# A new order of steps for a fused retention and Gelu MLP kernel: 1,332 steps listed anew, casts and copies given to other engines

## Chip, cores and metric

The kernel runs on one core of one Trainium2 chip. The metric is the device time of one launch in microseconds; lower is better.

## What is computed

Eight batches of eight heads, 576 positions, head size 64. Each head's attention has no softmax: scores are multiplied by a decay that depends on the distance, and the future is cut off. The result, 4608 tokens of 512 numbers, goes through a two-layer MLP with a tanh Gelu.

```python
scores = scale * np.matmul(q, k.transpose(0, 1, 3, 2))
gamma = 1.0 - 2.0 ** (-5.0 - np.arange(H, dtype=np.float32))
Dmat = np.where(rel >= 0, gamma[:, None, None] ** rel[None, :, :], 0.0)
attn = np.matmul(scores * Dmat[None, :, :, :], v)
x = attn.transpose(0, 2, 1, 3).reshape(B * S, H * D)        # 4608 x 512
h = x @ w_in                                                # 512 x 2048
g = 0.5 * h * (1.0 + np.tanh(c * (h + 0.044715 * h * h * h)))
out = g @ w_out                                             # 2048 x 512
```

Inputs and output are f32; the matmuls run in f16.

## The kernel before

**Tiling.** A unit u is a stretch of 128 positions of one batch (the fifth of each batch has 64): 40 units, u = 5 · batch + c. The retention is computed unit by unit with a running state, so a unit needs the scores inside it and the state of those ahead. The units of two batches (0, 2, 5, 7) are loaded in pairs ("wide"). The MLP takes the tokens in nine blocks t of 512. For t = 0 it is computed plainly; the second matmul from t = 1 on and the first from t = 6 on use Strassen's scheme, with seven products of half blocks in place of eight, whose sums and assembly fall to the other engines.

**Order.** Nothing is scheduled by a program at run time. The string `ORDER` is a list of steps; a loop at the end of the kernel calls one helper for each. Every engine gets its instructions in the order in which the steps stand in the list and works them off in that order, each waiting for its own inputs. PE, DVE, ACT and POOL have a list each, and SP a list of DMA issues; weights are issued from POOL's list. A step that waits holds up all that stands behind it on its engine. The last field of a step names the engine where there is a choice: v for DVE, a for ACT, g for POOL (for `t`, o and h name the PSUM ring).

| Step | Helper | What it does |
|---|---|---|
| L,u,n | load | SP: page n (q, k, v) of unit u |
| I,g and J,g | load_w_in, load_w_out | a chunk of w_in or w_out (256 KB in f16), cast by a DMA from POOL's list. N with fc 0 to 3 needs I,0 and I,1; 4 to 7 I,2 and I,3; 8 to 11 I,4 and I,5; 12 to 15 I,6 and I,7 |
| q, k, v | cast_q, cast_k, cast_v | page to f16, q and v with their decay |
| D,u | dma_T | SP: q and k transposed by a DMA (needs both casts) |
| t, y | pe_T, copy_T | the same by PE, and the copy out of PSUM |
| X, Y, R | wide_kv, wide_scores, wide_attend | PE's work for a wide pair |
| B,u,w | attend | scores of unit u and output of unit w on PE |
| m | masked | DVE: scores times the mask |
| a, o, z | state_sum, state_decay, state_16 | running state, its decay, its f16 copy |
| x | x_out | ACT: unit's output into xT, the MLP's input |
| N, F | mm1, gelu | w_in matmul (8 of 256 columns) and its Gelu |
| O, e | mm2, result | w_out matmul for t = 0 (and the last), copy out |
| P, E, Q | mm2_cols, result_cols, store | the last 128 tokens in three parts of columns |
| T, U, s, H | sum_b, sum_w, sum_x, sum_a | Strassen's sums, on DVE |
| W, V, S | product, assemble, store | Strassen's w_out products, assembly, store |
| A, l, f | product_h, part_h, gelu_h | Strassen's w_in products, parts, Gelu |
| K,n | busy | n filler matmuls on the identity (L1003), their result is not used |
| Z, g, c, w | zero, decay_rows, constants_short, table | constants; w runs one small Gelu |

**Buffers.** PSUM gives two banks to the ring "h" (N, A, t, K), two to "o" (O, W, t), and the rest to scores and outputs. A bank comes free when its reader is done: F for N, V for W, l and f for A. The f16 sums of Strassen's second matmul lie in eight tiles `ssum`, two sets of four, which `pair` hands out to the halves pr of each block t.

Of the kernel before, what the change touches and what calls it, by code (L numbers as in the profile page):

```python
# [1075 lines left out]
```

## Time and profile before

| What | Value |
|---|---|
| Time, median of 3 runs | 297.72 us (297.13 to 298.09) |
| Span of the profiled execution, first to last instruction | 293.9 us |
| The profiled execution's own time | not listed apart; at the median, 3.8 us lie around the span |
| Granted TensorE clock | 1.000 |
| DMA, mean | 169 GB/s, 49.79 MB in 136428 packets |
| PE's work in the span, useful matmuls and 36 fillers | 280.3 us busy |
| Fillers (L1003) | 10.4 us busy |
| Gelus (L765, L975) | 56.7 + 29.5 us on ACT |
| First and last instruction of N,0,2,0 and N,0,0,0 on PE | 21.30 to 23.21 us |
| Last matmul's end | 290.85 us |

The profile's busy time of an engine says how much it worked, not what it delays. PE is busy through most stretches of ten microseconds, so what counts is where it is not: in the head, until its inputs are there, and in single holes later. A wait of another engine costs something only where PE, in turn, waits for that engine. Rows of the timeline give start, duration, engine, line, operation, and in brackets the idle time ahead and what ended it.

### The profile page before, as it was taken

To read this page: it belongs to the slowest core of one execution; us is meant where nothing else is said; L and a number is where in the kernel's file an instruction comes from. 1 tells how busy PE (TensorE), PEld (TensorE's weight loads), DVE (VectorE), ACT (ScalarE), POOL (GpSimd) and SP (SyncE) were. 2 spreads that over 40 slices of the span, in tenths; PEclk is the share of its full clock that TensorE was granted. 3 is DMA by queue.
4 is the path that set the end of the run, shared out by engine and by line. 5 is a ranking of instruction groups with operands and counts; after the bars stand their busy time and mean duration, and the time that the engine had idled before them with its cause. 6 is when DMAs were issued, how large, how long until landed. Compare 5 with 4: busy or idle time off the path is not lost.

```text
span 293.9 us, 9639 instructions
## 1 busy us (share of the span) xinstructions
PE 280.3 (95%) x4064; PEld 235.2 (80%) x4064; DVE 216.6 (74%) x447; ACT 150.1 (51%) x289; POOL 109.6 (37%) x168
## 2 busy tenths in 40 slices
PE   3797999999999999999999999999999999999995
PEld 1355886667888888888888888888888788888874
DVE  7686753696865678576678699799889988977740
ACT  2144774334634543554553646546777587665411
POOL 5931910414351084163415544783467123000000
PEclk9999999999999999999999999999999999999999
DMA  7999999997979999989099978899498370002103
GB/s 212 283 236 250 217 220 211 214 179 162 248 142 228 178 186 220 230 206 210 23 235 214 196 166 178 187 204 153 131 195 208 75 205 7 36 8 102 74 25 121
DMA packets 136428, 49.79 MB, mean 169 GB/s; under 512 B 118208, under 2 KB 130880, under 8 KB 136384
## 3 DMA queue, kind: packets, MB, share of 16 engines
q1 hardware_dynamic: 132032, 44.97, 71.3%
q0 software_dynamic: 4352, 4.20, 8.5%
q8 instruction: 32, 0.52, 0.8%
q14 instruction: 12, 0.10, 0.1%
HBM read 36.70 MB, written 9.44 MB: 157 GB/s over the span
## 4 chain that ended last, share of the span: by engine, by line
PE 86%; POOL 5%; DMA 4%; DVE 3%; issue 1%; ACT 0%; POOLq 0%; ACTq 0%
PE bank L860 30%; PE bank L757 27%; PE bank L957 12%; PE bank L783 6%; DMA w_in_sb<-in_moe_w_in_dram 4%; PE sk L553 2%; PE x L529 2%; POOL w_in_sb L238 2%; PE sk L563 1%; PE x L574 1%; PE bank L987 1%; DVE pages L817 1%; POOL wide L269 1%; PE bank L493 1%; PE x L677 1%
## 5 line engine op out<-in xcount | busy, mean ns | idle before, releaser
L757 PE MATMUL bank<-xT,w_in_sb 128*128 128x256 f16 x768 | 94.4, 273 | 2.1 <-DMA w_in_sb<-in_moe_w_in_dram 2.1
L765 ACT ACTIVATE gT<-bank 128x512 f16<-128x512 f32 x96 | 56.7, 598 | 61.5 <-PE bank L757 59.7
L757 PEld LDWEIGHTS <-w_in_sb 128*128 128x128 f16 x768 | 73.8, 98 | 13.7 <-DMA w_in_sb<-in_moe_w_in_dram 2.7
L860 PEld LDWEIGHTS <-ssum 128*128 128x128 f16 x480 | 46.3, 98 | 6.5 <-issue 0.8
L269 POOL CAST sz<-s 64x256 f16<-64x256 f32 x48 | 24.4, 509 | 66.2 <-DVE s L713 45.9
L860 PE MATMUL bank<-tsum,ssum 128*128 128x256 f16 x360 | 46.0, 273 | 0.6 <-DVE ost L817 0.6
L860 PEld LDWEIGHTS <-gT 128*128 128x128 f16 x360 | 34.8, 98 | 4.5 <-issue 0.2
L424 POOL TENSOR_TENSOR qk<-pages,dec 128x512 f16<-128x512 f32 (+1 forms) x20 | 22.2, 1122 | 32.9 <-DMA pages<-in_q_dram 17.2
L860 PE MATMUL bank<-w_out_sb,gT 128*128 128x256 f16 x240 | 31.1, 273 | 0.0
L817 DVE TENSOR_TENSOR ssum<-gT 128x1024 f16<-128x1024 f16 x30 | 23.9, 798 | 3.9 <-ACT gT L765 3.5
L424 POOL TENSOR_TENSOR v<-pages,dec 128x512 f16<-128x512 f32 (+1 forms) x20 | 20.6, 1030 | 15.3 <-DMA pages<-in_v_dram 10.4
L817 DVE TENSOR_TENSOR ost<-u,bank 128x256 f32<-128x256 f32 x45 | 18.1, 416 | 9.5 <-PE bank L860 9.4
L817 DVE TENSOR_TENSOR ssum<-gT,ssum 128x1024 f16<-128x1024 f16 x30 | 23.4, 782 | 0.2
L691 DVE TENSOR_TENSOR ret<-sk,mask 128x512 f16<-128x512 f32 (+1 forms) x32 | 19.8, 618 | 4.3 <-PE sk L563 4.0
L957 PEld LDWEIGHTS <-pages 128*128 128x128 f16 x192 | 18.4, 98 | 2.8 <-issue 0.3
L957 PE MATMUL bank<-pages 128*128 128x256 f16 x144 | 20.3, 273 | 0.3 <-ACT pages L267 0.3
L783 PE MATMUL bank<-w_out_sb,gT 128*128 128x512 f16 x80 | 19.1, 380 | 0.0
L817 DVE TENSOR_TENSOR u<-u,bank 128x256 f32<-128x256 f32 x30 | 12.4, 415 | 8.7 <-PE bank L860 5.0
L713 DVE TENSOR_TENSOR s<-s,sk 128x256 f32<-128x256 f32 x36 | 14.9, 415 | 5.0 <-PE sk L563 4.0
L593 ACT ACTIVATE xT<-x 128x512 f16<-128x512 f32 (+1 forms) x25 | 14.3, 578 | 8.0 <-PE x L574 8.0
L817 DVE TENSOR_TENSOR hc<-hc,bank 128x512 f32<-128x512 f32 x21 | 14.4, 684 | 5.0 <-PE bank L957 2.3
L267 ACT COPY hc<-bank 128x512 f32<-128x512 f32 x19 | 11.1, 585 | 12.5 <-PE bank L957 12.4
(114 smaller groups left out, 425.8 us busy)
## 6 DMA issues: line engine op xcount, KB each, us to landing
out_dram<-ost SPq DMA_DIRECT2D x35, 256.0 KB, 3.4
pages<-in_q_dram SPq DMA_DIRECT2D x32, 256.0 KB, 4.7
pages<-in_v_dram SPq DMA_DIRECT2D x24, 256.0 KB, 4.1
pages<-in_k_dram SPq DMA_DIRECT2D x24, 256.0 KB, 4.3
pages<-in_k_dram SPq DMA_DIRECT2D x4, 512.0 KB, 5.2
pages<-in_v_dram SPq DMA_DIRECT2D x4, 512.0 KB, 6.0
w_in_sb<-in_moe_w_in_dram POOLq DMA_DIRECT2D x8, 256.0 KB, 9.8
w_out_sb<-in_moe_w_out_dram POOLq DMA_DIRECT2D x8, 256.0 KB, 10.6
```

The source lines that it names most:

```text
L267: nc.scalar.copy(out=o, in_=i)
L269: (nc.vector if eng == "v" else nc.gpsimd).tensor_copy(out=o, in_=i)
L424: eng.tensor_tensor(out=out, in0=s["raw"][:, i, 0:n], in1=dec[:, i // 2, s["j"], 0:n].unsqueeze(2).to_broadcast([128, n, D]), op=ALU.mult,)
L593: nc.scalar.activation(out=xT[:, :, o : o + G * (b - a)].rearrange("c p (h s) -> c p h s", s=G), in_=x[:, a:b].rearrange("c h p s -> c p h ...
L691: nc.vector.tensor_tensor(out=ret[:, :, 0:n], in0=now["two"][:, :, 0, 0:n], in1=mask.unsqueeze(1).unsqueeze(1).to_broadcast([128, 2, n, G] ...
L713: nc.vector.tensor_tensor(out=s32, in0=state[0], in1=kv, op=ALU.add)
L757: nc.tensor.matmul(hps[:, i, :], w_in_sb[:, ct, 128 * (fc + i) : 128 * (fc + i) + 128], xT[:, ct, TB * t % XR + lo : TB * t % XR + hi], st ...
L765: nc.scalar.activation(out=gTs[t][:, fc : fc + TB // (hi - lo), lo:hi], in_=h.pop((t, fc, lo)), func=AF.Gelu_apprx_tanh, bias=0.0, scale=1.0,)
L783: nc.tensor.matmul(ops[t, tcc], gTs[t][:, ft, 128 * tcc : 128 * tcc + 128], w_out_sb[:, ft, :], start=(ft == 0), stop=(ft == NFC - 1),)
L817: (nc.vector if eng == "v" else nc.gpsimd).tensor_tensor(out=out, in0=a, in1=b, op=op)
L860: nc.tensor.matmul(p["ps", bank][:, HN * col : HN * col + HN], a[:, k], b[:, k], start=(k == 0 and i in (1, 6)), stop=(k == HK - 1), skip_ ...
L957: nc.tensor.matmul(p["ps", bank][:, n], w[:, c, 128 * n : 128 * n + 128], x[:, c], start=(n == 0 and c == 0 and i in (1, 2, 5)), stop=(c = ...
```

## The change

`ORDER` is replaced as a whole. Both lists have the same 1,332 steps in kind and number (of `K` eleven in both, with 36 fillers before and 33 after), in another order. 120 other steps that have a choice name another engine. By kind: of z thirteen go from POOL to ACT, four from DVE to ACT, four from ACT to the others, five from POOL to DVE and eight from DVE to POOL; of k nine come to ACT and four leave it; of V nine copies go from ACT to DVE; of l five go to ACT and one leaves it; of q ten go to POOL and twelve to DVE; of v nine go each way. `w`, which stood among the steps of t = 5, stands in the head. J,0 to J,7 stand farther apart. D,9 stands ahead of the loads of units 10 to 14, and L,9,1 behind L,9,0.

In `pair`, the set of `ssum` is chosen by pr, not by the number of pairs so far.

The diff, with the list cut to its head and its end:

```diff
--- before.py
+++ after.py
 ORDER = """
-L,0,1 Z,1,v L,0,0 I,2,g L,0,2 L,2,1 L,2,0 Z,2,g q,0 k,0,g I,7,g K,4 K,4 K,4 K,3 K,4 t,0,q,h L,2,2
-L,4,1 c t,0,k,h I,1,g v,0,v X,0 y,0,k,v I,0,g I,3,g a,0,1 y,0,q,v Z,3,v k,2,g K,4 K,1 Y,0,1 t,2,k,o
-m,0,1 z,0,1,a I,6,g K,4 Y,0,0 a,1,1 q,2 L,4,0 K,4 t,2,q,h m,0,0 y,2,k,a y,2,q,v I,4,g K,1 R,0 I,5,g
-x,0 Y,2,1 L,5,0 x,1 i,4,v K,3 N,0,2,0 N,0,0,0 g o,1,1 m,2,1 L,5,1 Z,4,g v,2,v F,0,2,0 N,0,12,0 Y,2,0
-F,0,0,0 z,1,1,v N,0,4,0 L,5,2 X,2 k,4,g Z,5,v q,4 F,0,12,0 F,0,4,0 t,4,k,o a,2,1 t,4,q,o a,3,1
-y,4,q,a N,0,8,0 L,4,2 z,2,1,g L,9,1 N,0,10,0 F,0,8,0 k,5,g m,2,0 L,7,1 R,2 F,0,10,0 y,4,k,v B,4,-1
-q,5 x,3 x,2 N,0,14,0 L,7,0 t,5,q,o N,0,0,1 L,7,2 J,1,g F,0,14,0 N,0,6,0 y,5,q,v J,3,g t,5,k,o
-F,0,0,1 m,4 j,1,v J,0,g L,9,0 v,5,v J,2,g L,9,2 F,0,6,0 N,0,8,1 L,10,0 N,0,12,1 k,7,v X,5 y,5,k,a
-F,0,8,1 z,3,1,g F,0,12,1 v,4,v Y,5,0 a,5,1 m,5,0 a,6,1 N,0,4,1 N,0,6,1 F,0,4,1 q,7 F,0,6,1 t,7,k,o
-y,7,k,a N,0,2,1 J,5,g J,4,g N,0,14,1 F,0,2,1 J,6,g L,10,2 B,-1,4 F,0,14,1 x,4 Y,5,1 t,7,q,h y,7,q,a
-J,7,g m,5,1 N,0,10,1 v,7,v F,0,10,1 z,5,1,g R,5 x,5 Y,7,0 o,6,1 x,6 O,0,0 O,0,4 q,10,g L,11,1
-N,1,4,0 O,0,5 N,1,14,0 F,1,4,0 m,7,0 N,1,2,0 L,12,2 O,0,1 X,7 Y,7,1 F,1,14,0 F,1,2,0 L,15,1 k,9,a
-O,0,6 O,0,2 N,1,10,0 F,1,10,0 q,9,g O,0,3 L,11,2 N,1,6,0 D,9 F,1,6,0 m,7,1 Z,0,g k,11,a a,7,1 O,0,7
-e,0,0,v a,8,1 z,6,1,v O,0,12 T,1,0,v N,1,0,0 e,0,1,a F,1,0,0 z,8,1,g z,7,1,v N,1,8,0 O,0,13 L,10,1
-N,1,12,0 R,7 B,9,-1 H,1,0,3,v v,10,v F,1,8,0 x,8 O,0,8 L,11,0 L,12,1 O,0,14 j,5,v F,1,12,0 v,11,v
-T,1,1,v q,11 k,10,g x,7 O,0,15 N,1,6,1 H,1,0,1,v L,12,0 D,10 N,1,8,1 O,0,9 F,1,6,1 T,2,0,v v,9,v
-O,0,10 e,0,3,a T,3,0,v S,0,0 N,1,14,1 F,1,8,1 H,1,0,2,v m,9 L,14,1 B,10,9 k,12,a D,11 T,2,1,v O,0,11
-a,10,0 a,10,1 e,0,2,v N,1,12,1 L,13,2 F,1,14,1 L,13,0 x,9 N,1,10,1 m,10 F,1,12,1 T,3,1,v z,10,0,g
-B,11,10 q,12,g W,1,0,1 S,0,3 v,13,v a,11,0 V,1,0,0,a a,11,1 x,10 v,12,v W,1,0,6 L,14,0 F,1,10,1
-N,1,2,1 o,11,1 q,13,g F,1,2,1 T,4,0,v D,12 W,1,0,2 L,16,1 V,1,0,1,v N,1,4,1 N,1,0,1 S,0,2 V,1,0,2,a
-z,11,0,v F,1,4,1 z,10,1,g j,2,v m,11 S,0,1 N,2,0,0 B,12,11 q,14 a,12,0 H,1,0,4,v k,15,g F,1,0,1
-F,2,0,0 W,1,0,7 L,15,0 L,14,2 N,2,8,0 T,4,1,v N,2,4,0 V,1,0,3,v H,1,1,1,v L,13,1 z,12,0,g x,11
-k,16,g H,1,1,2,v W,1,0,4 W,1,0,5 F,2,8,0 L,17,0 a,12,1 N,2,6,0 L,17,1 V,1,0,5,v L,19,0 F,2,4,0
-k,13,g D,13 V,1,0,4,v F,2,6,0 m,12 N,2,14,0 v,14,v F,2,14,0 W,1,1,1 z,11,1,g V,1,1,0,a W,1,0,3
-V,1,0,6,v L,16,0 N,2,10,0 F,2,10,0 k,14,g W,1,1,6 V,1,1,1,v N,2,12,0 z,12,1,v L,16,2 B,13,12 x,12
-L,15,2 v,15,g D,14 q,15 W,1,1,2 H,1,1,3,v m,13 N,2,2,1 V,1,1,2,a W,1,1,7 F,2,12,0 N,2,2,0 V,1,1,3,v
...
+L,0,0 Z,3,v Z,2,v Z,1,g I,7,g K,0 L,0,2 L,0,1 q,0,g I,2,g v,0,v K,5 L,2,1 K,0 k,2,g K,4 K,4 K,4 K,4
+t,0,q,h K,4 w g k,0,v I,1,g y,0,q,v X,0 a,0,1 I,0,g t,2,k,o y,2,k,v L,2,0 z,0,1,a a,1,1 L,2,2 q,2
+t,0,k,h y,0,k,a Y,0,0 m,0,0 I,3,g I,6,g L,4,1 K,2 K,5 o,1,1 Y,0,1 m,0,1 t,2,q,h y,2,q,a I,4,g R,0
+x,1 x,0 K,1 Y,2,1 N,0,2,0 F,0,2,0 m,2,1 N,0,0,0 z,1,1,g F,0,0,0 v,2,g X,2 Y,2,0 N,0,4,0 F,0,4,0
+a,2,1 z,2,1,v a,3,1 N,0,14,0 F,0,14,0 m,2,0 R,2 x,2 x,3 L,4,0 I,5,g L,5,1 c N,0,12,0 i,3,a F,0,12,0
+L,5,0 N,0,6,0 k,4,v F,0,6,0 q,4 L,5,2 Z,0,v Z,4,v z,3,1,g J,0,g k,5,g t,4,k,o y,4,k,v N,0,0,1
+F,0,0,1 Z,5,g t,4,q,o y,4,q,a L,4,2 N,0,12,1 L,7,0 F,0,12,1 N,0,2,1 N,0,6,1 F,0,2,1 B,4,-1 m,4
+F,0,6,1 t,5,k,o y,5,k,v N,0,8,1 q,5,g F,0,8,1 J,1,g L,7,1 N,0,8,0 F,0,8,0 t,5,q,o y,5,q,a N,0,10,0
+F,0,10,0 i,1,g v,5,v X,5 a,5,1 a,6,1 Y,5,0 v,4,g N,0,14,1 F,0,14,1 N,0,4,1 F,0,4,1 B,-1,4 x,4 m,5,0
+Y,5,1 k,7,v z,5,1,a J,5,g N,0,10,1 q,7,g t,7,q,h t,7,k,o j,7,g m,5,1 R,5 O,0,4 y,7,q,v y,7,k,a Y,7,0
+x,6 O,0,0 m,7,0 L,7,2 J,2,g L,9,0 J,3,g x,5 F,0,10,1 N,1,8,0 F,1,8,0 L,9,1 N,1,4,0 v,7,v Y,7,1
+F,1,4,0 L,9,2 k,9,v q,9 J,6,g D,9 o,6,1 X,7 a,7,1 N,1,2,0 F,1,2,0 N,1,0,0 J,4,g T,1,0,v O,0,1 J,7,g
+N,1,14,0 T,3,1,v F,1,0,0 O,0,5 T,2,0,v N,1,6,0 F,1,6,0 F,1,14,0 O,0,6 O,0,2 O,0,7 L,13,0 e,0,1,a
+O,0,3 a,8,1 L,10,0 N,1,10,0 z,6,1,a N,1,12,0 O,0,8 q,10 O,0,9 L,10,1 k,10,v v,9,g T,1,1,v T,2,1,v
+O,0,10 m,7,1 L,12,1 F,1,10,0 O,0,11 z,7,1,g R,7 L,10,2 e,0,0,v L,11,0 L,11,1 B,9,-1 e,0,2,v j,1,v
+F,1,12,0 H,1,0,1,v O,0,12 O,0,13 O,0,14 k,11,a O,0,15 H,1,0,2,v L,14,0 m,9 z,8,1,v x,7 x,8 N,1,6,1
+v,10,v F,1,6,1 N,1,10,1 F,1,10,1 D,10 B,10,9 x,9 H,1,0,4,v e,0,3,a L,14,1 k,14,g L,12,0 a,10,0
+N,1,4,1 q,11,g N,1,14,1 F,1,4,1 H,1,0,3,v W,1,0,1 a,10,1 L,11,2 k,12,a N,1,0,1 V,1,0,0,a F,1,14,1
+F,1,0,1 z,10,0,a W,1,0,6 m,10 L,13,1 k,13,g L,14,2 N,1,2,1 q,12 q,13 F,1,2,1 D,11 v,11,g B,11,10
+x,10 S,0,1 V,1,0,1,v W,1,0,5 L,15,0 L,16,1 a,11,0 L,12,2 N,2,14,0 v,12,g F,2,14,0 W,1,0,2 V,1,0,2,a
+z,10,1,g N,2,2,0 F,2,2,0 S,0,0 z,11,0,g L,19,1 a,11,1 N,1,8,1 F,1,8,1 T,4,1,v o,11,1 T,3,0,v W,1,0,7
+j,4,a q,14 N,1,12,1 F,1,12,1 N,2,8,0 F,2,8,0 m,11 T,4,0,v D,12 H,1,1,1,v V,1,0,3,v q,15 V,1,0,4,v
+B,12,11 m,12 D,13 N,2,4,0 a,12,0 H,1,1,2,v a,12,1 z,11,1,g j,0,v F,2,4,0 S,0,2 L,13,2 D,14 W,1,0,4
+V,1,0,5,v W,1,0,3 L,15,2 x,11 L,21,1 L,15,1 L,17,1 L,20,1 N,2,12,0 V,1,0,6,v F,2,12,0 j,3,a L,17,0
+z,12,1,a N,2,6,0 F,2,6,0 L,16,0 W,1,1,1 N,2,10,0 v,13,v z,12,0,v B,13,12 a,13,0 F,2,10,0 k,15,g
...
 """
...
         if (t, pr) not in pairs:
             if not tsum:
                 sum_tiles()
-            n = len(pairs)
-            pairs[t, pr] = dict(s=[ssum[4 * (n % 2) + i] for i in range(4)])
+            pairs[t, pr] = dict(s=[ssum[4 * pr + i] for i in range(4)])
         return pairs[t, pr]
```

## Prediction

> **What bounds the kernel now.** I read the page's busy table first, then PE's waits, PE's busy time by stretches of ten microseconds, and the timeline of the stretches that showed a hole.
>
> ```profile
> span 293.9 us, 9639 instructions
> PE 280.3 (95%) x4064; PEld 235.2 (80%) x4064; DVE 216.6 (74%) x447; ACT 150.1 (51%) x289; POOL 109.6 (37%) x168
> ```
> PE's waits (who waited for whom: us, times, longest):
>
> ```profile
> PE bank L1003 <- DVE ident L364: 4.5, 1, 4.5
> PE bank L757 <- DMA w_in_sb<-in_moe_w_in_dram: 2.1, 2, 1.6
> PE bank L1003 <- DVE qkT L269: 1.9, 1, 1.9
> ```
> PE is the bound; the first and third wait are of fillers (L1003), the second is of real work. PE's list holds the same useful matmuls in both kernels, so the time is the moment at which the first hidden block N,0,2,0 starts, plus the same PE work, plus PE's holes after it, plus the tail. The stretches (us, busy and count of PE, PEld, DVE, ACT, POOL) show where the holes are:
>
> ```profile
> 20.00:30.00 10.00, 7.61 (x118) 5.62 (x118) 7.20 (x21) 5.50 (x9) 2.01 (x4) 1.00 1.17 240
> 30.00:40.00 10.00, 10.00 (x184) 8.87 (x183) 7.89 (x10) 6.86 (x13) 8.06 (x13) 1.00 1.02 222
> ...
> 220.00:230.00 10.00, 8.95 (x126) 7.58 (x124) 9.77 (x18) 6.86 (x13) 6.62 (x8) 1.00 0.73 172
> ...
> 250.00:260.00 10.00, 9.71 (x98) 8.47 (x96) 8.13 (x18) 6.17 (x13) 0.00 (x0) 1.00 0.07 27
> ```
> From 30 us on PE misses 1.05 + 0.29, and 0.08 and 0.02 in two stretches not shown: 1.44 us. The rest is in the head; the timeline of PE (start, duration, idle before) has it:
>
> ```profile
> 20.64 0.82 PE L1003 MATMUL bank<-ident 128*128 128x512 f16 x3
> 21.30 1.91 PE L757 MATMUL bank<-xT,w_in_sb 128*128 128x256 f16 x16
> 24.85 1.05 PE L757 MATMUL bank<-xT,w_in_sb 128*128 128x256 f16 x8 [1.64 <-DMA w_in_sb<-in_moe_w_in_dram]
> ...
> 28.61 1.70 PE L757 MATMUL bank<-xT,w_in_sb 128*128 128x256 f16 x14 [0.46 <-DMA w_in_sb<-in_moe_w_in_dram]
> ```
> The first N starts at 21.30. Then PE stands for 1.64 us until weight chunk I,6 lands (for N,0,12,0) and for 0.46 until I,5 lands (for N,0,10,0): 2.10 us. The chunks go out from POOL, and the pages from SP:
>
> ```profile
> 11.14 2.15 POOL L238 DMA_DIRECT2D w_in_sb<-in_moe_w_in_dram x3
> ...
> 14.33 2.16 POOL L238 DMA_DIRECT2D w_in_sb<-in_moe_w_in_dram x3
> ...
> 40.44 1.69 SPq L215 DMA_DIRECT2D pages<-in_q_dram  x1
> ...
> 51.62 1.61 POOL L424 TENSOR_TENSOR qk<-pages,dec 128x512 f16<-128x512 f32 x2 [13.10 <-DMA pages<-in_q_dram]
> ...
> 53.69 1.68 SPq L483 DMA_TRANSPOSE qkT<-qk  x1
> ```
> The first two rows are I,1 I,0 I,3 and I,6 I,4 I,5. I,6 took 24.85 − 14.33 = 10.5 us to land, I,5 28.61 − 15.8 = 12.8. The third row is L,10,0, used 11.2 us later.
>
> The span is 293.9; the profiled execution's own time is not listed apart, so I take the median, 297.72, of which 3.8 lies around the span.
>
> **The change, part by part.** *Start of the first N.* Fillers: 36 become 33, but all stand before the first N while PE waits for others. The opening ones, 19 in 5.92 us, become 21, so t,0,q comes at 10.26 + 2 × 0.2 = 10.65 at the latest from PE's side. q,0 goes from DVE (1.23) to POOL. No row has a 1024-wide multiply on POOL; 128x256 takes 0.67 and 128x512 1.20, so 1.2 + 2 × 0.53 = 2.3; bounds 1.2 and 2 × 1.2 = 2.4. POOL: masks end 6.5, Z,1 0.52, I,7 0.74, q,0 until 10.1, I,2 until 10.8, k,2 1.04 until 11.8, then I,1 I,0 I,3 I,6 I,4 at 0.72 each: I,0 goes out at 12.55 (before: 11.86), I,6 at 14.0 (before: 14.33). Copies: y,0,q on DVE until 12.2, z,0,1 (0.83) and y,0,k (1.01) on ACT until 14.5, so Y,0,0 at 14.5; DVE does y,2,k, a,1,1 and q,2 until 15.5, m,0,0 (1.22) until 16.7, o,1,1, m,0,1 until 18.5; R,0 then runs to 19.6 (before 19.8), x,1 and x,0 (1.09) end at 20.7, and N,0,2,0 can start 0.36 later as before: 21.05. Its weights: I,0 had landed by 21.30, at most 9.4 us after its issue, so by 12.55 + 9.4 = 21.95. Between 21.05 and 21.95 I take 21.4, since in the rows x, not the weights, was last.
>
> *Holes of the head.* Before, the third block asks for I,6 and I,7, the fifth for I,4. After, the third is N,0,4,0 (I,2 and I,3, long out) behind X,2 and Y,2,0; I,6 is needed by N,0,14,0 at 21.4 + 3 × 0.87 + 0.3 + 0.33 = 24.65. By the rows it lands between 24.5 and 25.5: a hole of 0 to 0.85, I take 0.3. I,4 and I,5 are first needed by N,0,8,1, 11.8 us of PE work after the first N, at 33.5. I,5 now stands on POOL behind z,1,1 (which waits for o,1,1, 17.3) and the wide v,2 (2.3): out at 20.6, landed by 20.6 + 12.8 = 33.4. No hole; 0.9 if v,2 starts a microsecond late. Head: before 21.30 + 2.10 = 23.40; after 21.4 + 0.3 = 21.7. Gain 1.7, bounds 2.35 and −0.35.
>
> *Gelu's table.* The load moves from 20.95 to ACT's wait after the constants, where ACT stands 6.2 us until 12.41. Before, it hid: 1.28 us to 22.23, the Gelu at 22.38, its matmuls just done at 22.2, and PE's next block waited for weights anyhow. Worth 0; with the cover of those weights gone it would be 0.15. The Trainium skill ("ScalarE: Activation LUTs", What ACT_TABLE_LOAD costs) adds about 1.38 us of drain to each switch, 2.66 together, which would put up to 1.4 us on ACT. The trace disagrees: x,0 ends at 20.94, the load starts at 20.95, and 0.15 follows it.
>
> *Other engines.* Counted from the list with row durations: 13 more z on ACT (0.81), 5 more k (0.6), 4 more l (0.585), 9 fewer V (0.37): ACT +12.5 us, to 55% of the span. POOL −11, DVE −2. ACT had waits of 60 us for PE in L765 alone, so it has room; DVE, at 9.77 of 10 where the late hole is, is not loaded more (in the 50 us of PE work around that hole the list holds 50.9 us of DVE rows before, 47.2 after). I keep the 1.44 us of holes; bounds 0 (they dissolve) and 3 (twice as many).
>
> *Tail.* Before it ends O, P,0, P,1, E,1 on ACT, Q,1; after O, P,0, P,2, E,2 on ACT, Q,2: both 128 columns. P,1 (after O,8,9) needs f,8,3,3 and f,8,2,2, two Gelus of 0.63 after V,8,0,5 and l,8,3,5; they end 0.2 us ahead of it. 0; bound 0.5. The ssum line takes 4·pr instead of 4·(n%2); pairs come in turn (pr 0, then 1), so it names the same tiles: 0.
>
> Sum: 297.7 − 1.7 = 296.0.
>
> **Rivals.** *(a) DVE stuck behind a page, slower.* D,9 now stands on SP ahead of all of L,10 to L,14, where before five of these loads went out first (40.44 to 53). D,9 waits for k,9 and q,9 on DVE, behind m,7,0 and v,7: Y,7,0 at 43.4, then 1.22 + 1.27 + 0.54 + 0.42 gives 47.2; D,9 takes 1.3 to issue, L,13,0 and L,10,0 follow, out by 49.5. q,10 on DVE waits for it, and behind it queue k,10, T,1,1, T,2,1 and m,7,1 (0.69 + 0.68 + 0.84 + 0.73 + 1.22 = 4.2). R,7 needs m,7,1 and comes 39.2 us of PE work after the first N, at 60.6 (the same count puts before's R,7 at 60.9; its row says 60.65). So it costs from a landing of 56.4 on; at 58.1 the gain of 1.7 is gone, at 59.0 the kernel is slower by 0.9. With the page's median of 4.7 it lands at 54.2; with the 11.2 of the row above at 60.7: 4.3 us lost, 300.3. Against it: by then fewer weights compete. *(b) POOL's chain late, no change.* If DVE and POOL exclude each other, q,0 waits for v,0 on DVE (1.5, to 8.5) and ends at 10.8; I,0 goes out at 13.25 and lands by 22.65: the first N moves by 1.25, 297.2, with I,6 late too up to 297.9. For it: a DVE ssum of 1.42 us (mean 0.78) beside a POOL L424 at 226 us; against: the wide v on DVE (L439) took 1.50 instead of q's 1.23 beside POOL's cast at 8.66, a stretch of 0.27 only. The Trainium skill ("SBUF — State Buffer", Who interferes with whom) says an operation of DVE with two SBUF inputs and one of GpSimd that reads SBUF block each other whole; by it this case is the likely one. The two rows split on it. *(c) The late holes dissolve*, as DVE has less there: 296.0 − 1.4 = 294.6. *(d)* The new order has late holes of its own, twice the old: 297.5 and more.
>
> **How the numbers follow.** Forecast 0.50 (0.45 of it a gain over 0.9 us), (a) 0.20, (b) 0.15, (c) 0.10, (d) 0.05 counted slower. A measurement of this kernel tells about 0.3%, 0.9 us. Faster 0.45 + 0.10 = 0.55; same 0.05 + 0.15 = 0.20; slower 0.25. The range starts at 294.8, near (c), and ends at 299.3, which takes in (b), (d) and the milder half of (a).
>
> **What would show it.** Right: first N at 21.0 to 22.0, no wait of PE for w_in_sb above 0.9, R,7 about 60.6 with no hole before it, ACT near 163 us busy. Wrong: PE idle before L665 or L677 near 60 us with DVE's q,10 waiting for pages (a); first N at 22.5 or later (b); new holes of PE after 75 us (d); a tail longer than before's 3.0 us after the last matmul.

## The result, and the profile after

After takes 293.19 us in the median of four runs (292.71 to 294.13), before 297.43 beside it: a ratio of 0.9871 (0.9842 to 0.9900). Run again beside the experiments (e16 below) the same list took 294.94 in six runs, ratio 0.9937 (0.9915 to 0.9958). The two intervals do not meet. A likely reason stands in the runs: in the first comparison all four had a mean granted clock of 0.999 or 1.000, in the second five of six had 0.993 or 0.994, and the sixth, at 1.000, took 293.22. All ten together have a median of 294.18; before, over the 108 runs that stood beside the experiments, 296.75. So the change is worth some 2.6 us, 0.9%, and 3.5 us where the clock stays up. The forecast was 296.0, a gain of 1.7, with a range from 294.8: the direction was right, the size too small, and 293.19 lies below the range.

One run of e6 (300.27) and three of e17 (296.06 to 296.53) lie over 1.5% above the quickest run of their kernel, and no ratio, median or table here counts them.

From the page of after, the lines that answer to those of before:

```profile
span 291.0 us, 9645 instructions
PE 279.8 (96%) x4061; PEld 235.4 (81%) x4061; DVE 212.9 (73%) x444; ACT 163.3 (56%) x316; POOL 95.0 (33%) x144
```

ACT has the 13 us more that were forecast, POOL 15 less, PE the same work. PE's waits after (lines below `pair` have moved up by one, so the fillers' L1003 is L1002 and L860 is L859):

```profile
PE bank L1002 <- DVE ident L364: 4.5, 1, 4.5
PE sk L636 <- ACT qkT L267: 1.5, 1, 1.5
PE bank L757 <- DMA w_in_sb<-in_moe_w_in_dram: 0.9, 1, 0.9
PE x L677 <- DVE ret_wide L644: 0.5, 2, 0.3
PE bank L859 <- DVE ost L817: 0.4, 1, 0.4
```

The waits for weights (2.1 us before) are one of 0.9, and it stands ahead of the first N. The stretches of ten microseconds, in the columns of before:

```profile
20.00:30.00 10.00, 8.94 (x167) 7.50 (x167) 5.15 (x11) 5.61 (x11) 6.09 (x14) 1.00 1.17 256
30.00:40.00 10.00, 10.00 (x170) 8.58 (x169) 5.74 (x8) 6.75 (x13) 8.25 (x9) 1.00 1.15 266
...
220.00:230.00 10.00, 10.00 (x94) 8.96 (x92) 8.76 (x19) 6.90 (x14) 0.79 (x2) 1.00 0.42 88
...
250.00:260.00 10.00, 10.00 (x94) 8.95 (x93) 7.35 (x14) 6.38 (x13) 0.00 (x0) 1.00 0.07 28
```

The late holes (8.95 and 9.71 busy before) are not there; beside them, from 220 to 230 us, DVE fell from 9.77 to 8.76 of ten and POOL from 6.62 to 0.79. In before these holes were three, two behind DVE and one behind ACT:

```profile
225.67 0.60 PE L957 MATMUL bank<-xT,w_in_sb 128*128 128x256 f16 x4 [0.42 <-DVE pages L817]
...
228.65 1.03 PE L860 MATMUL bank<-tsum,ssum 128*128 128x256 f16 x8 [0.64 <-DVE ost L817]
...
253.77 0.60 PE L957 MATMUL bank<-pages 128*128 128x256 f16 x4 [0.29 <-ACT pages L267]
```

The head of after on PE, POOL, and then SP and DVE further on:

```profile
21.35 1.92 PE L757 MATMUL bank<-xT,w_in_sb 128*128 128x256 f16 x16 [0.85 <-DMA w_in_sb<-in_moe_w_in_dram]
...
60.61 0.61 PE L665 MATMUL x<-qkT,sz 128*128 128x128 f16 x8
```
```profile
7.99 2.85 POOL L439 TENSOR_TENSOR wide<-pages,decw 128x1024 f16<-128x1024 f32 x1
...
12.53 3.59 POOL L238 DMA_DIRECT2D w_in_sb<-in_moe_w_in_dram  x5
```
```profile
46.49 1.30 SPq L483 DMA_TRANSPOSE qkT<-qk  x1
...
53.80 0.69 DVE L424 TENSOR_TENSOR qk<-pages,dec 128x512 f16<-128x512 f32 x1 [1.46 <-DMA pages<-in_q_dram]
```

The first N starts at 21.35 and R,7 (L665) at 60.61, both as forecast. q,0 on POOL took 2.85 us, not 2.3. D,9 goes out at 46.49; q,10 waits 1.46 us for its page and starts at 53.80, ahead of the 56.4 from which rival (a) would cost.

**A measure for the rest.** Holes alone do not say when PE fell behind, since fillers and a slow clock also fill its busy time. So I count, from the stretches of each matmul line, the useful matmuls done by a time T, multiply each count by the spacing of that line in an unbroken run (0.109 us for 128x256, 0.2165 for 128x512, less for the small ones) and subtract from T. This lag is time that was not useful PE work; it stays level while PE is full. It is good to about 0.3 us. A hole counts some 0.16 us more in it than in the timeline: a row of 128x256 lasts 0.27 us while the next starts 0.109 behind it, and the idle time in brackets begins only at the row's end. The three late holes of before are 1.34 us by their brackets and 1.8 by the starts of the matmuls.

| Lag in us at T = | 40 | 100 | 160 | 220 | 260 | 280 |
|---|---|---|---|---|---|---|
| before | 20.3 | 20.3 | 20.3 | 20.1 | 22.2 | 22.3 |
| before again (e1) | 20.2 | 20.2 | 20.2 | 20.0 | 22.1 | 22.3 |
| after | 18.3 | 18.6 | 18.9 | 18.9 | 19.1 | 19.5 |
| after again (e16) | 18.4 | 18.7 | 18.5 | 18.5 | 18.6 | 19.0 |

Two steps make the gain: 1.8 to 2.0 us in the head, and 2.1 us between 220 and 260 us, of which after loses 0.1 to 0.2. New holes give back 0.6 us by 220 us in the first profile of after, 0.1 in the second, and in both some 0.3 more from 260 to 280 us.

### The profile page after: what moved, and what is told of

The parts are those of the page before. It is cut to its first block, busy times and chain, and to the rows that moved or that the text cites. A ratio compares the mean times of both kernels' runs of the same rounds, so it can differ in the third digit from the quotient of the medians.

```text
span 291.0 us, 9645 instructions
## 1 busy us (share of the span) xinstructions
PE 279.8 (96%) x4061; PEld 235.4 (81%) x4061; DVE 212.9 (73%) x444; ACT 163.3 (56%) x316; POOL 95.0 (33%) x144
## 4 chain that ended last, share of the span: by engine, by line
PE 84%; DVE 8%; DMA 3%; POOL 3%; issue 1%; ACT 1%; POOLq 0%; DVEq 0%
PE bank L859 29%; PE bank L757 26%; PE bank L956 13%; PE bank L783 6%; DMA w_in_sb<-in_moe_w_in_dram 3%; DVE ssum L817 2%; PE sk L553 2%; PE x L529 2%; PE sk L563 1%; PE bank L986 1%; PE x L574 1%; DVE s L713 1%; POOL wide L439 1%; DVE sz L269 1%; POOL w_in_sb L238 1%
## 5 line engine op out<-in xcount | busy, mean ns | idle before, releaser
L859 PEld LDWEIGHTS <-ssum 128*128 128x128 f16 x480 | 46.4, 98 | 6.5 <-issue 0.5
L859 PE MATMUL bank<-tsum,ssum 128*128 128x256 f16 x360 | 45.7, 273 | 0.5 <-DVE ost L817 0.4
L859 PEld LDWEIGHTS <-gT 128*128 128x128 f16 x360 | 35.1, 98 | 4.1
L424 POOL TENSOR_TENSOR v<-pages,dec 128x512 f16<-128x512 f32 (+1 forms) x19 | 19.5, 1028 | 37.7 <-DMA pages<-in_v_dram 22.1
L859 PE MATMUL bank<-w_out_sb,gT 128*128 128x256 f16 x240 | 31.1, 273 | 0.0
L817 DVE TENSOR_TENSOR ssum<-gT 128x1024 f16<-128x1024 f16 x30 | 22.4, 751 | 3.5 <-ACT gT L765 1.9
L817 DVE TENSOR_TENSOR ost<-u,bank 128x256 f32<-128x256 f32 x45 | 18.4, 416 | 8.3 <-PE bank L859 8.1
L691 DVE TENSOR_TENSOR ret<-sk,mask 128x512 f16<-128x512 f32 (+1 forms) x32 | 19.7, 617 | 6.3 <-PE sk L563 6.3
L424 POOL TENSOR_TENSOR qk<-pages,dec 128x512 f16<-128x512 f32 (+1 forms) x15 | 14.9, 997 | 24.8 <-DMA pages<-in_q_dram 11.9
L817 DVE TENSOR_TENSOR ssum<-gT,ssum 128x1024 f16<-128x1024 f16 x30 | 22.3, 742 | 0.4
L956 PE MATMUL bank<-pages 128*128 128x256 f16 x144 | 21.0, 273 | 0.1
L956 PEld LDWEIGHTS <-pages 128*128 128x128 f16 x192 | 18.3, 98 | 2.7 <-issue 0.4
L267 ACT CAST sz<-s 64x256 f16<-64x256 f32 x40 | 16.1, 402 | 7.7 <-DVE s L711 5.9
L269 POOL CAST sz<-s 64x256 f16<-64x256 f32 x26 | 12.2, 468 | 25.1 <-DVE s L711 12.4
L783 PE MATMUL bank<-w_out_sb,gT 128*128 128x512 f16 x80 | 18.8, 379 | 0.0
```

Source lines behind the costliest of these rows:

```text
L267: nc.scalar.copy(out=o, in_=i)
L269: (nc.vector if eng == "v" else nc.gpsimd).tensor_copy(out=o, in_=i)
L424: eng.tensor_tensor(out=out, in0=s["raw"][:, i, 0:n], in1=dec[:, i // 2, s["j"], 0:n].unsqueeze(2).to_broadcast([128, n, D]), op=ALU.mult,)
L691: nc.vector.tensor_tensor(out=ret[:, :, 0:n], in0=now["two"][:, :, 0, 0:n], in1=mask.unsqueeze(1).unsqueeze(1).to_broadcast([128, 2, n, G] ...
L783: nc.tensor.matmul(ops[t, tcc], gTs[t][:, ft, 128 * tcc : 128 * tcc + 128], w_out_sb[:, ft, :], start=(ft == 0), stop=(ft == NFC - 1),)
L817: (nc.vector if eng == "v" else nc.gpsimd).tensor_tensor(out=out, in0=a, in1=b, op=op)
```

## The experiments

Each was timed in three or five rounds beside the kernel before; the ratio is to that, with its interval.

| Run | Median us | Ratio | Lag at 40 | 100 | 220 | 260 | 280 |
|---|---|---|---|---|---|---|---|
| e1 before again | 297.08 | 1.0009 (0.9986 to 1.0033) | 20.2 | 20.2 | 20.0 | 22.1 | 22.3 |
| e2 new head | 297.64 | 1.0018 (0.9996 to 1.0040) | 18.8 | 21.0 | 21.6 | 23.8 | 24.0 |
| e3 new rest | 294.92 | 0.9935 (0.9911 to 0.9958) | 22.0 | 21.9 | 21.7 | 22.0 | 22.3 |
| e4 new engines | 309.35 | 1.0412 (1.0388 to 1.0435) | 22.9 | 25.3 | 30.5 | 34.9 | 35.5 |
| e5 old blocks renamed | 295.26 | 0.9944 (0.9925 to 0.9964) | 19.0 | 19.3 | 19.7 | 21.5 | 21.8 |
| e6 new blocks renamed | 297.21 | 1.0001 (0.9971 to 1.0031) | 23.8 | 24.2 | 24.7 | 24.8 | 24.9 |
| e7 old engines | 316.22 | 1.0645 (1.0603 to 1.0688) | 21.9 | 26.4 | 35.2 | 38.4 | 39.9 |
| e8 sums behind | 297.82 | 1.0034 (1.0014 to 1.0055) | 20.3 | 20.3 | 20.4 | 23.7 | 24.0 |
| e9 renamed, and new rest | 292.95 | 0.9863 (0.9831 to 0.9894) | 19.1 | 19.1 | 19.8 | 20.0 | 20.4 |
| e10 new from t = 6 | 299.19 | 1.0073 (1.0046 to 1.0101) | 20.9 | 20.9 | 25.3 | 25.6 | 25.6 |
| e11 new engines from t = 6 | 299.29 | 1.0091 (1.0060 to 1.0122) | 20.9 | 20.9 | 21.7 | 25.3 | 25.4 |
| e13 new order from t = 6 | 303.56 | 1.0243 (1.0193 to 1.0294) | 21.0 | 21.0 | 24.4 | 27.7 | 27.7 |
| e12 weights in order | 295.71 | 0.9967 (0.9945 to 0.9989) | 21.7 | 21.9 | 22.4 | 22.5 | 22.9 |
| e14 q,0 on DVE | 293.83 | 0.9887 (0.9857 to 0.9917) | 18.6 | 18.8 | 18.9 | 19.0 | 19.6 |
| e15 short head | 293.18 | 0.9872 (0.9843 to 0.9902) | 19.5 | 19.7 | 19.7 | 19.9 | 20.5 |
| e16 after again | 294.94 | 0.9937 (0.9915 to 0.9958) | 18.4 | 18.7 | 18.5 | 18.6 | 19.0 |
| e17 short head, weights held back | 291.58 | 0.9852 (0.9810 to 0.9894) | 17.2 | 17.4 | 17.8 | 17.9 | 18.3 |
| e18 the same again | 292.94 | 0.9879 (0.9839 to 0.9919) | 17.1 | 17.3 | 17.9 | 17.9 | 18.3 |

The lag is of the profiled run alone, which can lie some 2 us from the median.

**e1, the base.** The list before, unchanged.

> The kernel before, unchanged, for more spans and a second trace. Theory A (the profiled run of before was a quick one): its spans lie near 295.5, with 1.7 to 2 us around them as in the runs of the changed kernel, and the new trace has more than 1.44 us of holes on PE after 30 us. Theory B (the runs of before have more around the span): spans near 293.9, 3.5 to 4 us around them, and the same 1.44 us of holes.

Twelve runs spread from 295.74 to 298.74. Their time is 1.7 to 1.9 us above their span, not 3.8: the profiled run of before (span 293.9) was a run of about 295.6, 2 us quicker than its median. The new trace has the same late holes (8.94 busy of ten from 220 to 230 us).

**e5 and e6, the order of the first blocks.** Only the first eight N and F of t = 0, first half, are renamed; places, engines and chunks stay.

```diff
 e5, list before:
-N,0,2 N,0,0 N,0,12 N,0,4 N,0,8 N,0,10 N,0,14 N,0,6
+N,0,2 N,0,0 N,0,4 N,0,6 N,0,12 N,0,14 N,0,8 N,0,10
 e6, list after:
-N,0,2 N,0,0 N,0,4 N,0,14 N,0,12 N,0,6 N,0,8 N,0,10
+N,0,2 N,0,0 N,0,12 N,0,4 N,0,8 N,0,10 N,0,14 N,0,6
```

> The old list with one thing changed: the first eight blocks of N and F for t = 0 ask for the columns of w_in in the order of their chunks' arrival (2, 0, 4, 6, 12, 14, 8, 10 in place of 2, 0, 12, 4, 8, 10, 14, 6). Theory A (the late chunks I,4 to I,6 alone are the head's cost, and PE's list then moves up whole): the waits for w_in_sb of 1.0 to 3.5 us go and the time falls by 1.5 to 2.5 us, to about 294.8. Theory B (the next wait comes up behind it, a unit's page or its casts, as the old list asks for them no earlier): less than 0.7 us below before.

> The new list with the old order of these eight blocks (third 12, fourth 4, fifth 8, sixth 10). I,5 stays behind v,2 on POOL, out at 21.8. Theory A: PE waits for I,6 at the third block and for I,5 at the sixth until about 31, 2.5 to 3.5 us above the changed kernel, which is 296 to 297. Theory B (the order of the blocks is not what matters): within 0.7 us of the changed kernel.

e5 has no wait for w_in_sb and gains 0.56%, 1.7 us: this one edit is the forecast's term for the head. e6 loses the whole gain: with the old names, after's blocks come to I,6 and I,5 before these have landed. Two rows of PE's timeline in e6:

```profile
25.14 1.92 PE L757 MATMUL bank<-xT,w_in_sb 128*128 128x256 f16 x16 [0.71 <-DMA w_in_sb<-in_moe_w_in_dram]
...
31.17 2.18 PE L757 MATMUL bank<-xT,w_in_sb 128*128 128x256 f16 x11 [2.77 <-DMA w_in_sb<-in_moe_w_in_dram]
```

**e2, e3 and e9, head and rest apart.** The cut is at R,7, 60 us in: what stands ahead of it from one list, all that is left from the other. e9 is e3 with the renaming of e5.

```diff
 e2: steps ahead of R,7 of the list after, then the rest of the list before
 e3: steps ahead of R,7 of the list before, then the rest of the list after
 e9: as e3, with
-N,0,12 N,0,4 N,0,8 N,0,10 N,0,14 N,0,6
+N,0,4 N,0,6 N,0,12 N,0,14 N,0,8 N,0,10
```

> The new list up to R,7 (60 us), then the old list for all that is left. Theory A (two parts that add up): the head brings 1.7 us as worked out beforehand, so about 1.7 us below before, and the other 2.5 us are in the rest. Theory B (all in the head): 4.2 us below before. Theory C (the head's gain is given back by old holes later): no change.

> The old list up to R,7, then the new list for all that is left. Theory A (two parts that add up): 2.5 us below before, with the old waits for w_in_sb of 2.1 us still there and at most 0.8 us of holes on PE after 75 us. Theory B (all in the head): no change. Theory C: 4 us or more below before.

> The list before up to R,7 with its first eight hidden blocks renamed so that the chunks out first are used first, then the list after. Theory A: the change has two separate gains, one in the head (the renaming alone gave a ratio of 0.9944) and one in the rest (the new rest alone gave 0.9935); together 0.9944 x 0.9935 = 0.988, that is 293.5 us, as after itself (0.9871); PE has no wait for w_in_sb over 0.9 us and the time that is not useful PE work grows by less than 1.3 us from 40 us to the end. Theory B: an earlier head only runs into a later limit of the new rest; then 294.9 us as with the new rest alone, and new holes of PE after 60 us that add up to over 1 us.

e2 has the gain of the head at 40 us (18.8) and loses it where the lists are joined: PE waits 1.48 us at 78.67 for a Gelu on ACT that stands behind a copy waiting for a store. It says nothing on the head's worth, only that the old rest does not fit behind the new head. e3 loses only 0.3 us between 220 and 260 us, and gains 0.65%. e9 has both: 0.9863, where 0.9944 x 0.9935 is 0.988, and after itself has 0.9871 and 0.9937. Two such parts are enough for the whole gain, and they add up.

**e8, e10, e11 and e13, the late loss.** e8 moves two sums of t = 6 on DVE behind an assembly that PE waited for; e10 takes order and engines of after from A,6,0,1 on (197 us, where the two lists are joined: the seam), e11 only the engines (30 steps), e13 only the order.

```diff
 e8, list before:
-L,39,0 H,6,1,3,v q,37,g ... l,7,1,1,a H,6,1,1,v V,6,0,3,v ... V,6,0,4,v a,37,0
+L,39,0 q,37,g ... l,7,1,1,a V,6,0,3,v ... V,6,0,4,v H,6,1,1,v H,6,1,3,v a,37,0
```

> The old list with two of DVE's part sums, H,6,1,3 and H,6,1,1, moved from ahead of l,7,0,5 and V,6,0,3 to behind V,6,0,4, so that what PE waits for at 225 and 228 us comes off DVE 0.8 to 1.5 us earlier. Theory A (the order on DVE makes the late hole): the hole of 1.05 us between 220 and 230 goes, 1.0 to 1.6 us below before. Theory B (DVE is simply full from 215 to 245, 9.6 of 10): the hole turns up somewhat later, no change.

> The list before up to its step A,6,0,1 (184 us of PE work), then all that is left in the order and with the engines of the list after. Theory A: before loses its late 2 us by how its own steps of t = 6 to 8 stand; then they are gone here, ratio 0.9935, 295.2 us, PE's lag flat from 200 to 260 us, while the 2.1 us of weight waits in the head stay. Theory B: the loss is set up earlier, by what the list before has left undone on DVE when t = 6 begins; then it stays, ratio 1.00, 297.1 us, with holes of PE between 215 and 235 us as before.

> The list before in its own order; only the steps from A,6,0,1 on take the engines of the list after (30 steps: among them z and k of units 31 to 38 from POOL to ACT, four V from ACT to DVE, five l from DVE to ACT). Theory A: the late loss comes from POOL's casts and DVE's slower beside them, so engines alone take it away: ratio 0.994, 295.3 us, DVE's ssum rows near 0.75 us. Theory B: it is the order (what stands ahead of the V and the page adds on DVE), and engines that do not fit the order do harm, as in the run with all new engines: ratio 1.00 to 1.01, 297 to 300 us, holes of PE as large or larger between 215 and 260 us.

> As the run with the new rest from t = 6 (the list before up to A,6,0,1, then the order of after), but all steps keep the engines of the list before. The seam near 197 us costs what it cost there (4.4 us of lag between 180 and 220 us, ratio 1.0073). Theory A: the order alone takes the late loss away: lag flat from 220 to 260 us as there, ratio near 1.007. Theory B: the order needs its engines (it puts copies of V on DVE early and casts on ACT where ACT is free): lag grows by 2 us or more from 220 to 260 us, ratio 1.012 or higher.

From 220 to 260 us the lag grows by 2.1 us in before, 3.3 in e8, 0.3 in e10, 3.6 in e11 and 3.3 in e13. In e8 the same two holes come 0.7 us later:

```profile
226.36 0.60 PE L957 MATMUL bank<-xT,w_in_sb 128*128 128x256 f16 x4 [0.42 <-DVE pages L817]
229.37 1.03 PE L860 MATMUL bank<-tsum,ssum 128*128 128x256 f16 x8 [0.66 <-DVE ost L817]
```

The stretches of e11, with the new engines on the old order, show more holes than before's:

```profile
220.00:230.00 10.00, 9.57 (x132) 8.26 (x131) 9.29 (x20) 7.19 (x14) 4.89 (x7) 1.00 0.89 204
230.00:240.00 10.00, 8.85 (x128) 7.59 (x127) 8.29 (x17) 5.86 (x12) 3.68 (x7) 1.00 0.70 116
...
250.00:260.00 10.00, 9.41 (x95) 8.16 (x94) 8.62 (x20) 6.45 (x13) 0.00 (x0) 1.00 0.07 29
```

So neither the order nor the engines of after take the late loss away alone; both together do. In e8 two sums on DVE stood later, and no hole went: the two kept their size, and a new one of 0.72 us, behind DVE, came at 239.46. That fits a DVE that is short of time there, but its share alone does not decide: in e11 PE misses 1.15 of ten with DVE at 8.29. Which steps of the full set matter is not settled. The seam of e10 cost 4.4 us, of which only 2.9 is holes; what the rest is stands under the hardware below.

**e4 and e7, engines and order exchanged as a whole.** e4 is the list before with after's engines, e7 the list after with before's.

> The old order of steps, each on the engine that the new list names. Theory A (the order makes the gain): within 1 us of before or slower, since the old order was not made for these engines. Theory B (moving work from POOL to ACT makes the late gain, as DVE's f16 sums are held up less by POOL): 1 to 2.5 us below before, with the mean of DVE's ssum rows down from 0.79 to about 0.75.

> The new order of steps, each on the engine that the old list names. Theory A (order and engines are fitted to each other; neither alone is the gain): several us slower than the changed kernel, as the new engines in the old order were 12 us slower than before. Theory B (the order alone is the gain): within 1 us of the changed kernel, 293 to 294.

They cost 4% and 6%. Behind the opening fillers PE has some 20 waits in e4 and 25 in e7, none over 1.8 us, for casts, copies, sums, Gelus and transfers. An order without its engines is worth less than either whole; neither run divides the gain.

**e12, e14, e15, e17 and e18, what holds the first N of after.** All are the list after with another head. e12 sends the chunks out in the order of use and moves copies and masks; e14 moves one multiply; e15 and e17 rebuild the head. The steps of e17 up to the second block, against after:

```diff
-L,0,0 Z,3,v Z,2,v Z,1,g I,7,g K,0 L,0,2 L,0,1 q,0,g I,2,g v,0,v K,5 L,2,1 K,0 k,2,g K,4 K,4 K,4 K,4
-t,0,q,h K,4 w g k,0,v I,1,g y,0,q,v X,0 a,0,1 I,0,g t,2,k,o y,2,k,v L,2,0 z,0,1,a a,1,1 L,2,2 q,2
-t,0,k,h y,0,k,a Y,0,0 m,0,0 I,3,g I,6,g L,4,1 K,2 K,5 o,1,1 Y,0,1 m,0,1 t,2,q,h y,2,q,a I,4,g R,0
-x,1 x,0 K,1 Y,2,1 N,0,2,0 F,0,2,0 m,2,1 N,0,0,0
+L,0,0 Z,3,v Z,2,v I,1,g K,0 L,0,2 L,0,1 I,0,g q,0 Z,1,g I,2,g v,0,v K,5 L,2,1 K,0 K,4 K,4 w
+t,0,q,h y,0,q,a K,5 k,0,v g I,3,g X,0 a,0,1 z,0,1,a t,0,k,o y,0,k,v K,3 k,2,g I,7,g I,6,g L,2,0 L,2,2
+Y,0,0 a,1,1 m,0,0 t,2,k,o y,2,k,a L,4,1 K,4 Y,0,1 m,0,1 q,2 o,1,1 K,4 R,0
+x,1 x,0 z,1,1,g I,4,g v,2,g I,5,g K,5 N,0,2,0 F,0,2,0 t,2,q,o y,2,q,a N,0,0,0
 e14:
-q,0,g
+q,0
```

> The list after with another head: weight chunks out in the order in which their blocks come (I,1 I,0 I,2 I,3 I,7 I,6 I,4 I,5, the first two ahead of the wide q on POOL), the copy of k ahead of z,0,1 on ACT, both masks of unit 0 ahead of q,2 on DVE, the transposition of q,2 behind R,0, and the third pair of blocks swapped with the second pair. Theory A: the first N is held by the chain through y,0,k, the masks and R,0 as much as by its weights; with both earlier it starts at 19.8 to 20.3 in place of 21.35, and the time is 1.0 to 1.5 us below after: ratio to before 0.982 to 0.984. Theory B: the weights' total traffic is the limit of the head, so the blocks behind the first two wait for I,3 or I,6 as much as was gained: ratio 0.987, as after, with waits of PE for w_in_sb over 1 us.

> The list after with one step changed: the wide q of unit 0 goes back from POOL to DVE, ahead of the wide v. Theory A (DVE and POOL exclude each other in these multiplies): the pair takes 2 x 1.23 us on DVE alone, q ends near 8.2 in place of 10.84, the five chunks behind it go out up to 2.9 us earlier, v,0 near 9.4; the first N loses its 0.85 us wait for w_in_sb and starts at 21.0, held by x alone: 0.3 us gained, ratio to before 0.986. Theory B: the first N is held only by the weights' traffic; it starts when it did, ratio 0.987. A start before 20.9 speaks for a chain through the masks that begins with q,0.

> The list after with a head of its own: both wide multiplies of unit 0 on DVE (q first), all weight chunks ahead of that work on POOL in the order in which the blocks come (I,1 I,0 I,2 I,3 I,7 I,6 I,4 I,5), the copy of q on ACT and that of k on DVE, both masks of unit 0 ahead of q,2, 30 fillers in place of 33 but spread so that PE stands nowhere above 0.3 us. By row durations t,0,q comes at 8.2, X,0 at 10.3, the masks at 12.5 and 13.8, R,0 ends at 15.6, x at 16.7. Theory A (the chain of copies and masks holds the head): the first N starts near 17 to 18, the lag at 40 us falls from 18.3 to 15 to 16, and the time is 2 to 3 us below after: ratio to before 0.977 to 0.981. Theory B (the DMA traffic holds it: 16 queues are full from 6 us on): the pages of k and of unit 2 come late, or blocks wait for I,3, I,6 or I,5, in sum as much as was gained: ratio 0.987 or above, with waits of PE for w_in_sb or DVE for pages over 1 us.

> The list after as it is. All theories: a ratio to before of 0.985 to 0.990, as in its first comparison (0.9871); the first N at 21.2 to 21.7; the time that is not useful PE work 18.3 to 18.8 us at 40 us and below 20 at 280 us.

> The short head once more, with I,4 and I,5 held back behind z,1,1 and v,2 on POOL, the transposed k of unit 0 into the other PSUM ring so that it does not wait for a filler's bank, the constants of g in DVE's wait ahead of X,0, and 32 fillers. Theory A (the order of the transfers is what cost the last run its gain): v,2 starts near 20 in place of 22.4, the first N at 18.4 to 19.3, PE's holes between it and 30 us add up to less than 1 us in place of 2.3, the lag at 40 us is 16.5 to 17.5, and the time 1 to 2 us below after: ratio to before 0.980 to 0.984. Theory B (the traffic as a whole is the limit: the pages of units 0 and 2 and the weights together): v,2 or the blocks of I,6 and I,4 wait as long as was gained; lag at 40 us 18.3 or more, ratio 0.987 or above.

> The same kernel as the run before. Theory A (the transfers' order is the limit and is now right): most runs lie at 291.4 to 292.5, ratio 0.980 to 0.985. Theory B (the landing times of the 16 shared queues vary from run to run, and a head that is earlier than its data loses the gain in the runs in which they come late): the runs spread over 4 us or more again, the median is 293 to 295.5, ratio 0.985 to 0.994, as for after itself, and a profile of a slow run shows PE waiting in the head for w_in_sb or DVE or POOL for pages.

e12 was 1.5 us behind after's ten runs, by none of its theories: the wide v on DVE was locked out by POOL's wide q for 1.7 us, PE worked only 1.5 of the 3.4 us up to 20.51, its granted clock fell to half there, and the fillers I had left ahead of the first N took double (it started at 24.24). In e14, with q,0 on DVE, the first N is held by x alone. Its row, then those of e15 (PE, POOL) and e17:

```profile
21.63 1.91 PE L757 MATMUL bank<-xT,w_in_sb 128*128 128x256 f16 x16 [0.51 <-ACT xT L586]
```
```profile
19.28 1.03 PE L757 MATMUL bank<-xT,w_in_sb 128*128 128x256 f16 x8
...
24.36 0.45 PE L619 MATMUL x<-wide,wide 64*64 64x64 f16 x32 [1.06 <-POOL wide L439]
```
```profile
22.41 1.90 POOL L439 TENSOR_TENSOR wide<-pages,decw 128x1024 f16<-128x1024 f32 x1 [7.35 <-ACT gT L765]
```
```profile
17.92 1.03 PE L757 MATMUL bank<-xT,w_in_sb 128*128 128x256 f16 x8
```

e14's x ended at 21.57 and the first N came 0.06 later. In after x ended at 20.97 and the first N came 0.38 later: there the weights were last, by 0.3 us. That e14's first N is no earlier than after's says nothing against its theory A, for its fillers were slower: the 21 opening ones, which start at 4.52 in both, took 7.50 us against 6.88, and t,0,q came at 11.85 against 11.24. The early ones take 0.43 us each and the later ones 0.22, and the moment of the change lies between 7.9 and 10.7 us in the traces (9.1 in after, 9.6 in e16, 10.1 in e14); the profile's clock column shows 1.00 on either side of it. So starts of the first N in single traces compare to about half a microsecond only. e15 started 2.1 us earlier, and at 40 us it was 1.2 us behind after: all eight chunks went out ahead of unit 2's v, whose multiply on POOL came 2.4 us later than after's (19.99), and PE stood for it. e17 holds two chunks back; there the same multiply waits for its page and comes at 20.01. It starts 3.4 us earlier than after and keeps 1.1 us of that at 40 us. So the chain of copies and masks holds the first N of after to 21.0 and the weights hold it to 21.35; for a first N ahead of 19.3 us (e15, e17) the order of the transfers counts as well.

The ratios do not follow as clearly. The two comparisons of the short head hold nine runs from 290.58 to 294.35, median 292.16; after's ten have 294.18. But their ratios, 0.9852 and 0.9879, lie within the interval of after's first, 0.9842 to 0.9900, so no version is shown to beat after, though the quickest run is 2 us below after's quickest. Both profiles are of runs of 291.4 and 291.6 us, so what the longer ones wait for was not seen. And after itself missed what was expected of it in e16, a ratio of 0.985 to 0.990, with 0.9937.

## Where the prediction was right, and why it was wrong

**The head: right, and a little small.** The first N was forecast at 21.4 and came at 21.35; a hole of 0.3 was forecast, none came in the first profile and 0.19 in the second. The gain was 1.7 by the sum, 1.8 to 2.0 by the lag, 1.7 by e5. That the start fits to 0.05 us is in part luck, for several terms were off and cancelled. t,0,q came at 11.24, not at 10.65 at the latest: the opening fillers took 6.88 us. q,0 on POOL ended at 10.84, as rival (b) had it, and I,0 went out at 13.25, as there; but it landed within 8.1 us, not the 9.4 of the sum, so the mechanism of (b) was real and cost 0.3 us, not 1.25. And the weights were last, not x. The 0.36 us from x to the first N, taken over from before, were fillers there (PE's row at 20.64, for 0.82, runs up to N); without them the step is 0.06, as e14 shows.

**The late holes: the step that failed.** I kept 1.44 us of holes and gave rival (c), that they dissolve, a chance of 0.10. They did dissolve: 1.34 us of the holes lie between 220 and 260 us, where the lag of before grows by 2.1 and that of after by 0.2. I had a sign of it in the count of DVE's rows around the hole (50.9 us before, 47.2 after), and used it only to say that things would not get worse. Where DVE is busy 9.77 of ten and PE waits for it, 3.7 us less work is a reason to expect smaller holes; holes that hang on one list order are not a constant that a new list inherits. That the new list removes them, and needs its order and its engines together for it, is shown by e3, e10, e11 and e13; which of its steps do it stays open. The price was too small as well, since 1.44 counts the brackets alone, and the range began at 294.8, above (c)'s own 294.6. With (c) as the likeliest case and the lag's 2.1 as its price, the sum would have been 297.7 − 1.7 − 2.1 = 293.9, against 294.18 over all ten runs.

**The base.** 3.8 us around the span were a mistake of 2 us; it is 1.7 in nearly all runs. The forecast in spans, 293.9 − 1.7 = 292.2, stands against 291.0 and 290.5. The sum started from 297.7, the median of three runs, 1.0 above that of the 108. From 296.75 it would have been 295.05, and 292.95 with the late holes at 2.1, against 293.22 for the runs of after whose clock stays up.

**Gelu's table: nothing, as forecast.** e5 takes the cover of the weights away and leaves the load where it was: it runs from 22.00, and the first Gelu comes at 23.29, 1.14 us after its matmuls began, against 1.08 in before and 1.09 in after. PE has no hole behind it.

**Engines.** ACT 163.3 us for the 163 forecast, POOL 15 less for 11, DVE 4 less for 2. The tail after the last matmul is 3.1 us before and 3.0 after.

**Rivals.** (a) did not come: D,9 went out at 46.49 (the terms given for it add up to 46.85, not 47.2), q,10 ran at 53.80, T and m,7,1 behind it were done at 57.9, 2.7 us ahead of R,7 at 60.61, with no hole there. (b) came by its mechanism and (c) whole, as said above; (d) came to 0.6 us in one profile of after and 0.1 in the other (lag from 40 to 220 us).

## What to carry to other kernels

When PE is full except in a few holes, a new order should be priced hole by hole: ask which engine ends each and whether it still has that much to do there, and do not carry old holes over. Order and engine choice are one decision: half of either list cost up to 6%. An earlier start is kept only if the transfers behind it come in the same order, and if PE is never left so empty on the way that its clock falls.

## What the runs showed of the hardware

**A hole of PE can cost double, through its clock.** At the seam of e10 PE waits 2.16 and 0.67 us; then the granted clock is at half for some 3.4 us. The stretches (PE's busy time first, then the others, PEclk third from the end) and PE's rows:

```profile
200.00:202.00 2.00, 1.25 (x16) 1.02 (x16) 2.00 (x5) 0.61 (x3) 0.83 (x1) 1.00 0.87 198
202.00:204.00 2.00, 2.00 (x60) 1.58 (x57) 0.84 (x4) 0.56 (x1) 0.24 (x1) 0.56 1.30 206
204.00:206.00 2.00, 2.00 (x13) 1.47 (x12) 1.35 (x2) 1.24 (x3) 1.82 (x2) 0.59 0.94 209
```
```profile
200.07 0.60 PE L956 MATMUL bank<-pages 128*128 128x256 f16 x4 [2.16 <-ACT qk L267]
...
202.83 1.04 PE L956 MATMUL bank<-pages 128*128 128x256 f16 x4
```

Four matmuls take 1.04 us in place of 0.60, with PE busy throughout. The two stretches at half clock lose 2 x 0.44 + 2 x 0.41 = 1.7 us, the part of e10's 4.4 that the holes leave over. One such spell in a run of 291 us is a mean clock of 1 − 1.7 / 291 = 0.994, two 0.988: the values that the runs list, with none of before's between 0.994 and 0.997. The Trainium skill ("TensorE: Matmul & The Clock Gate", Part 1: The HAM clock gate) has half rate in steps of a free-running window of 3.41 us, which would be 1.7 us each by an estimate; the trace agrees. It gives a whole idle window as the trigger, and there the runs differ: a hole of 2.2 us stood ahead of the drop here; the one of 1.87 us in the head of before is followed by one in some runs (0.65 and 0.50 from 14 to 18 us in e5) and not in others; and in e12 no hole was over 0.94. In the 3.41 us ahead of the drop PE had worked 1.48 us in e10, 1.51 in e12 and 1.54 in e5, so it was not idle; but in before it worked 1.55 from 11.28 to 14.70 and no drop follows, so no limit can be read from these. In e6 the hole of 2.77 us, too, is followed by half clock, from 31.57 to 34.98.

What a spell costs differs from list to list:

| Runs | Clock 0.997 to 1 | Clock below |
|---|---|---|
| before, 108 | 296.70 (68 runs) | 296.81 (40 runs) |
| e5, 12 | 295.14 (5 runs) | 295.35 (7 runs) |
| after, 10 | 293.22 (5 runs) | 294.99 (5 runs) |
| short head (e17, e18), 9 | 291.58 (7 runs) | 294.03 (2 runs) |

In before it is nearly free: where the profile of a run with before's head shows it (e1, e5, e10) it lies in the head, and in e1 and e10 blocks there wait for weights as well. That this cover is what makes it free is not shown, since e5 has no such wait and loses only 0.2 us. Where the spell lies in after's runs was not seen, since both its profiles have a clock of 1.

**DVE and POOL shut each other out in these multiplies.** In e12 the two wide multiplies start 0.04 us apart:

```profile
8.12 1.90 POOL L439 TENSOR_TENSOR wide<-pages,decw 128x1024 f16<-128x1024 f32 x1
```
```profile
8.16 2.94 DVE L439 TENSOR_TENSOR wide<-pages,decw 128x1024 f16<-128x1024 f32 x1 [1.68 <-DMA pages<-in_v_dram]
```

POOL, first, takes its 1.90; DVE's 1.23 end 1.08 after POOL's. In after DVE was first, by 0.14: it took 1.23 and POOL 2.85. The Trainium skill ("SBUF — State Buffer", Who interferes with whom) says that a DVE instruction with two SBUF inputs contends with a GpSimd instruction that reads SBUF, and that the ports they share are an exclusive lock; both cases agree. So does the row that the prediction counted against it: in before POOL's cast ran from 7.96 to 9.08, and DVE's multiply, started at 8.66, ended at 10.16, again 1.08 us behind POOL. It was a stretch of 0.27 only because the two met for no longer. e14 puts both multiplies on DVE, where they take 2.33 us together; its first N is no earlier, since the fillers ahead of t,0,q set its start.
